# Attention rounds of a fused attention and MoE kernel: the quads' projections one round later, key steps alone in the first two rounds, and unused products behind the routing table

## The chip, the cores and the metric

The kernel runs on one core of a Trainium2 chip. The time is the device time of one execution in microseconds. Three runs of the kernel before took 760.27, 762.58 and 767.11 us; the median is 762.58. A further execution was profiled: it took 762.83 us, and its span from the first to the last instruction is 761.1 us.

## The reference, cut to what matters

Three layers follow each other. The part that the change touches is the first, a linear attention with the feature map exp(p), exp(-p) of a projection p from which its largest magnitude is taken; and, at its end, the start of the second, a mixture of 8 experts with one expert per token.

```python
def phi(x):                                   # x is q or k: 4 batches, 8 heads, 576 tokens, 64
    proj = np.einsum('bhsd,df->bhsf', x, w_phi)                # 64 -> 128 features
    proj = proj - np.max(np.abs(proj), axis=-1, keepdims=True)
    return np.concatenate([np.exp(proj), np.exp(-proj)], axis=-1)
q_p, k_p = phi(q), phi(k)
kv = np.einsum('bhsf,bhsd->bhfd', k_p, v)
z = np.sum(k_p, axis=2)
num = np.einsum('bhsf,bhfd->bhsd', q_p, kv)
den = np.einsum('bhsf,bhf->bhs', q_p, z)[..., None] + 1e-06
x = num / den                                 # 2304 tokens of 512, then:
logits = normalized(x) @ normalized(expert_emb).T / tau       # 8 experts; argmax picks one
...
out[mask] = gate_w[mask, None] * (np.maximum(x[mask] @ w1[e], 0.0) @ w2[e])   # per expert
h = np.maximum(np.maximum(x @ m1, x @ m2), x @ m3); return h @ w_out          # third layer
```

## The kernel before

The attention is written out by hand in program order; every engine runs its instructions in that order, and waits on semaphores. Its loop runs over 18 *rounds* (`for r in range(R1)`, line 488). Two streams run through the rounds:

- **Key steps.** The keys and values are cut into 18 steps (`steps`): for each batch two row blocks (`u`) by two halves of the heads (`hq`), and for each pair of batches one step for the rows that are left. Step n goes through `k_T` (PE transposes, ACT copies to `kT`), `k_proj` (PE products with w_phi into two PSUM banks `pskp`), `k_exp` (DVE takes the largest magnitude `mk` and subtracts it to `pk`; ACT makes two exps, `kp`), `k_pair` (DVE adds the two rows of a pair, `zr`) and `k_acc` (PE sums key-value products `kv` and key sums `z`). In round r, step r is summed, step r+1 projected and step r+2 transposed.
- **Quads of queries.** The queries are cut into 16 quads (4 per batch; two share one load `q`). A quad goes through `q_T` (PE transposes, DVE copies to `qT`), `q_front` (PE products `psqf`, ACT copies them to `pq`, POOL's all-reduce over the partitions gives the maxima `mq`), `q_sub` (DVE subtracts), `q_exp` (ACT, to `ex`) and, once its batch's keys are summed, `q_num` and, every second quad, `q_den`. The dictionary `at` says in which round a quad's `q_num` stands: quads 0 to 7 in rounds 5 to 12, quads 8 on from round 14. `LEAD = 4` puts `q_front` four rounds ahead of it, `q_exp` three, and `q_T` five.

Names of PSUM tiles made by `bank(...)` share five banks in turn (tag `W`), so a PE instruction that writes a bank waits until the reader of the tile five places back is done. `idle(n)` issues n products of zeros into a bank that nobody reads; before the loop 11 of them stand ahead of the first transposes, 8 in round 0. `prep_experts` (the generator `pe`) normalizes the expert embeddings `emb` on DVE ahead of the first key step and transposes them in round 2 (`ps_en`, to `enp`). Loads are issued on SP in program order (`load_u` keys and values, `load_r` the left rows, `load_q`), a few first ones on ACT; w_phi is loaded twice, into both halves of `w2`.

Behind the loop comes the tail: the last quads, then the routing generator `chain` (`Routing.blocks`): PE products `rt_n`, `rt_before`, and 18 products of 18 columns, `rt_tok`, in three groups, each waiting for a table `R` that DVE makes. DVE casts the result to the token list `s2t`, and POOL gathers token rows `xs` by it from DRAM, where the x tiles were stored. The expert layer begins with `fill(12)` twice (line 1035): 24 unused products of 512 columns, then the transposes of the gathered rows (`turn`, line 933).

Of the kernel before, what the change touches and what calls it, by code (L numbers as in the profile page):

```python
# [46 lines left out]
def attention(tc, q, k, v, w_phi, expert_emb, tau, x_d, lraw, ssq, ident, io, kx, ex_, rt, ids):  # L47
# [17 lines left out]
    LEAD = 4  # L65

    with ExitStack() as ctx:
# [12 lines left out]
        def load_u(b, u, parts=(0, 1)):  # L80
            if (b, u) not in kvu:
                pool = wk if (2 * b + u) % 3 == 1 else io
                kvu[b, u] = pool.tile([P, 2, H, 2, D], F32, tag="kv", name=f"kv{b}_{u}", bufs=1 if pool is wk else 2)
            d = kvu[b, u]
            for i in parts:
                src, dst = ((k, kt), (v, vt))[i]
                for h0, h1 in ((0, 4), (4, 8)) if b == u == i == 0 else ((0, 8),):
                    nc.sync.dma_start(
                        out=d[:, i, h0:h1].rearrange("p h r d -> p h (r d)"),
                        in_=src[b, h0:h1, u * 256:(u + 1) * 256, :].rearrange("h (p r) d -> p h (r d)", r=2),  # L90
                    )
                dst[b, u] = d[:, i]
# [44 lines left out]
        nc.scalar.dma_start(out=w2[D:P], in_=w_phi)  # L137
# [8 lines left out]
        load_kv(3)  # L146
        kld = [4]
# [4 lines left out]
        def idle(n):  # L152

            ps = bank("warm")
# [3 lines left out]
        idle(WARM[4])  # L158
# [14 lines left out]
        def prep_experts():  # L173
# [7 lines left out]
            nc.vector.tensor_tensor(ern, ern, esq, op=ALU.mult)  # L181
            nc.vector.tensor_scalar(ern, ern, 1e-6, taub, op0=ALU.add, op1=ALU.mult)
# [130 lines left out]
        def q_T(v):  # L313
            m, g = divmod(v, 2)
            if g == 0 and m + 1 < 2 * B:
                load_q(m + 1)
            qT[v] = wk.tile([P, 4, 2, QR], F32, tag="qT", name=f"qT{v}")
            for rp in range(2):
# [5 lines left out]
                nc.vector.tensor_copy(qT[v][:, :, rp, :], psv)  # L324

# [158 lines left out]
        k_proj(0)  # L484
        for _ in k_exp(0):
            pass
        fin = None
        for r in range(R1):

            if r + LEAD in at:  # L490
                q_front(at[r + LEAD])
            if r + LEAD - 1 in at:
                m, g = divmod(at[r + LEAD - 1], 2)
                for pp in range(2):
                    q_exp(m * NP_ + 2 * g + pp)
            k_proj(r + 1)

            k_T(r + 2)
            ke = k_exp(r + 1)
            next(ke, None)  # L500
            if r and r + LEAD + 1 in at:
                q_T(at[r + LEAD + 1])
# [11 lines left out]
            for _ in pe if r == 2 else ():  # L514
                pass
            if r == 0:
                idle(8)
            if r + LEAD in at:
                q_sub(at[r + LEAD])
# [26 lines left out]
            if r == 0:  # L546
                q_T(at[LEAD + 1])
            k_pair(r + 1)
# [52 lines left out]
        ex_.low(1, 1)  # L601
        for _ in chain:
# [802 lines left out]
```

## Time and profile before

| | |
|---|---|
| median of the runs | 762.58 us (760.27 to 767.11) |
| profiled execution: time, span | 762.83 us, 761.1 us |
| busy: PE, DVE, ACT, POOL | 734.4, 403.4, 353.4, 135.6 us |
| granted TensorE clock, mean of the span | 0.993 |
| DMA, mean over the span | 100 GB/s |
| attention (to the end of rt_tok) | about 206 us |

How to read it: a timeline row names an engine, a source line, the operation and its tiles; a number in brackets is the time that the engine stood idle just before, with what ended it. A row with x32 covers 32 records; a product of fp32 leaves two records. The granted clock is 1.00 at the upper of its two levels and 0.50 at the lower one. An idle time costs something only where the engine is the one that sets the pace, and in this kernel that is mostly PE.

### The profile page before, as it was taken

The numbers are of one execution on the slowest core, as the hardware profiler recorded it, in microseconds if no ns is written. First come the engines' busy times: TensorE is split into PE (matmuls) and PEld (weight loads), VectorE is DVE, ScalarE is ACT, GpSimd is POOL, SyncE is SP. The second block draws the span as 40 slices with busy tenths as digits, with TensorE's granted clock in tenths as the row PEclk, the third lists the DMA queues.
The fourth block names the chain that finished last, engine by engine and source line by source line (L and its number), as shares of the span: only waits on it lengthen the run. The fifth ranks groups of instructions, "written<-read, shape, count | busy, mean of one in ns | idle before, by whom it ended". The sixth has DMA issues, their size and how long they took to land. (4 is left out here: it accounts for less than half of the span.)

```text
span 761.1 us, 13360 instructions
## 1 busy us (share of the span) xinstructions
PE 734.4 (96%) x5492; PEld 605.0 (79%) x5492; DVE 403.4 (53%) x619; ACT 353.4 (46%) x600; POOL 135.6 (18%) x112
## 2 busy tenths in 40 slices
PE   7899999899999999999999999999999999999995
PEld 6566665665599889998899997888888887888884
DVE  7876667677755554665365588667512222222220
ACT  4676757776755545755275565433231131012111
POOL 1654224442052101005500000000020011002002
PEclk9999999999999999999999999999999999999998
DMA  8644533026147642473334514341010000001001
GB/s 191 156 104 99 112 95 86 16 84 222 72 115 281 229 156 80 176 223 112 113 113 146 190 59 164 122 157 57 2 56 28 1 28 31 0 1 57 0 1 55
DMA packets 59741, 75.93 MB, mean 100 GB/s; under 512 B 11632, under 2 KB 41976, under 8 KB 59648
## 3 DMA queue, kind: packets, MB, share of 16 engines
q1 hardware_dynamic: 55712, 64.53, 27.2%
q0 software_dynamic: 3456, 9.46, 3.6%
q8 instruction: 70, 1.15, 0.7%
q10 hardware_dynamic: 480, 0.61, 0.2%
q14 instruction: 23, 0.19, 0.1%
HBM read 65.12 MB, written 9.46 MB: 98 GB/s over the span
## 5 line engine op out<-in xcount | busy, mean ns | idle before, releaser
L1260 DVE TENSOR_TENSOR raw<-raw,b 128x512 f32<-128x512 f32 x36 | 24.8, 688 | 130.4 <-PE b L1252 126.8
L341 POOL PARTITION_ALL_REDUCE mq<-pq x32 | 69.0, 2206 | 97.5 <-ACT pq L339 91.4
L1281 POOL DMA_INDIRECT out_dram<-raw,c2t x18 | 17.8, 989 | 362.5 <-ACT raw L1280 332.5
L1006 PE MATMUL b<-hxH,wL 128*128 128x304 f32 (+2 forms) x256 | 80.3, 313 | 0.0
L1006 PE MATMUL b<-hxH,wH 128*128 128x304 f32 (+2 forms) x256 | 80.2, 313 | 0.0
L1006 PE MATMUL b<-hxL,wH 128*128 128x304 f32 (+2 forms) x256 | 80.0, 313 | 0.0
L995 DVE SCALAR_TENSOR_TENSOR hxL<-b,hxH 128x512 fp32r<-128x512 f32 x64 | 42.3, 686 | 68.0 <-ACT hxH L994 67.6
L994 ACT ACTIVATE hxH<-b 128x512 fp32r<-128x512 f32 x64 | 38.2, 608 | 44.2 <-PE b L987 40.0
L987 PE MATMUL b<-xeH,w1hi 128*128 128x304 f32 (+2 forms) x256 | 57.2, 317 | 0.0
L987 PE MATMUL b<-xeH,w1lo 128*128 128x304 f32 (+2 forms) x256 | 55.7, 313 | 0.0
L1006 PEld LDWEIGHTS b<-hxL,wH 128*128 128x128 f32 x256 | 48.4, 189 | 2.7 <-DVE hxL L995 0.2
L1006 PEld LDWEIGHTS b<-hxH,wH 128*128 128x128 f32 x256 | 48.4, 189 | 2.6 <-issue 0.2
L1006 PEld LDWEIGHTS b<-hxH,wL 128*128 128x128 f32 x256 | 48.5, 189 | 2.5
L987 PEld LDWEIGHTS b<-xeH,w1lo 128*128 128x128 f32 x256 | 42.0, 189 | 2.9 <-ACT xeH L941 0.4
L987 PEld LDWEIGHTS b<-xeH,w1hi 128*128 128x128 f32 x256 | 41.9, 189 | 2.3
L958 DVE TENSOR_TENSOR wL<-raw,wH 128x2048 fp32r<-128x2048 f32 x16 | 36.6, 2289 | 11.4 <-ACT wH L957 11.4
L987 PE MATMUL b<-xeL,w1hi 128*128 128x304 f32 (+2 forms) x128 | 40.1, 313 | 0.0
L987 PE MATMUL b<-xeL,w1lo 128*128 128x304 f32 (+2 forms) x128 | 39.5, 312 | 0.0
L927 POOL DMA_INDIRECT xs<-x_d,s2t x18 | 21.8, 1212 | 98.6 <-PE b L933 67.6
L1264 ACT CAST m2h<-raw 128x512 fp32r<-128x512 f32 x12 | 7.4, 620 | 67.6 <-DVE raw L1260 67.6
L228 DVE TENSOR_REDUCE mk<-pskp 128x4 f32<-128x512 f32 x36 | 24.7, 685 | 24.8 <-PE pskp L217 24.8
L1252 PE MATMUL b<-xeH,wH 128*128 128x512 f32 x96 | 37.3, 389 | 0.0
(254 smaller groups left out, 1765.3 us busy)
## 6 DMA issues: line engine op xcount, KB each, us to landing
raw<-in_moe_w_dram SPq DMA_DIRECT2D x32, 1024.0 KB
raw<-in_moe_w_dram SPq DMA_DIRECT2D x18, 512.0 KB
q<-in_q_dram SPq DMA_DIRECT2D x8, 576.0 KB
kv<-in_v_dram SPq DMA_DIRECT2D x8, 512.0 KB
x_d<-x SPq DMA_DIRECT2D x16, 256.0 KB
kv<-in_k_dram SPq DMA_DIRECT2D x7, 512.0 KB
raw<-in_moe_w_out_dram SPq DMA_DIRECT2D x6, 512.0 KB
kv<-in_k_dram SPq DMA_DIRECT2D x2, 256.0 KB
```

The lines of the kernel that those rows point to most:

```text
L228: nc.vector.tensor_reduce(m, psb[j], axis=AX.X, op=ALU.max, apply_absolute_value=True)
L341: nc.gpsimd.partition_all_reduce(mx.rearrange("p a b -> p (a b)"), d.rearrange("p a b -> p (a b)"), P, ReduceOp.absmax)
L927: self.nc.gpsimd.indirect_dma_start(out=d, out_offset=None, in_=self.x_d, in_offset=bass.IndirectOffsetOnAxis(ap=idx, axis=0))
L958: self.nc.vector.tensor_tensor(L, r, H.bitcast(F32), op=ALU.subtract)
L987: nc.tensor.matmul(ps[:, 0:N], w, x[:, k, 0:N], start=(i == 0), stop=(i == 11))
L994: nc.scalar.activation(hH, ps, AF.Relu)
L995: nc.vector.scalar_tensor_tensor(hL, ps, 0.0, hH.bitcast(F32), op0=ALU.max, op1=ALU.subtract)
L1006: nc.tensor.matmul(ps[:, 0:N], w[i][:, c:c + P], h[f // 4][:, f % 4, 0:N], start=(f == 0 and q == 0), stop=(f == 7 and q == 2))
L1252: nc.tensor.matmul(b, w, y[k], start=(k == 0 and q == 0), stop=(k == 3 and q == 2))
L1260: nc.vector.tensor_tensor(m, m, b, op=ALU.max)
L1264: nc.scalar.copy(hH, m)
L1281: nc.gpsimd.indirect_dma_start(out=self.out, out_offset=bass.IndirectOffsetOnAxis(ap=rt.c2t[:, t:t + 1], axis=0), in_=o, in_offset=None)
```

## The change

1. **Quads one round on.** `LEAD` goes. In round r the quad is `qv = r - 2`: its `q_front` and `q_sub` stand there, the `q_exp` of quad r-3, the `q_T` of quad r-1. For quads 0 to 7 that is a round later than before; quads 8 to 15 keep their rounds, and round 9, which had no projection, now has quad 7's.
2. **The first two rounds.** Key projections 0 and 1 and transposition 2 stand ahead of the loop; round 0 projects step 2 in the middle of `k_exp(1)`, behind the 8 unused products, and transposes step 3 at its end. Round 1 has `k_pair(1)` in the middle of `k_exp(2)`, and quad 0's `q_T` at its end.
3. **Expert embeddings.** `prep_experts` stops ahead of the step that needs tau; the scaling follows in round 1, the transposes in round 2.
4. **Loads.** The second half of w_phi is loaded on SP behind the first half of the first keys, no longer on ACT. Queries 1 are loaded ahead of the loop, queries m+2 behind the last transposition of queries m.
5. **Unused products.** Those ahead of the first transposes and of round 0 write the bank `kv1` and not one of the five; 12 new ones stand behind the third group of `rt_tok`.

```diff
-    LEAD = 4
...
+                    if h1 == 4:
+                        nc.sync.dma_start(out=w2[D:P], in_=w_phi)
...
-        nc.scalar.dma_start(out=w2[D:P], in_=w_phi)
...
+        load_q(1)
...
-        def idle(n):
-            ps = bank("warm")
+        def idle(n, early=False):
+            ps = ps1.tile([P, 512], F32, tag="kv1", name="warm") if early else bank("warm")
...
-        idle(WARM[4])
+        idle(WARM[4], True)
...
             nc.vector.tensor_tensor(ern, ern, esq, op=ALU.mult)
+            yield
             nc.vector.tensor_scalar(ern, ern, 1e-6, taub, op0=ALU.add, op1=ALU.mult)
...
-            if g == 0 and m + 1 < 2 * B:
-                load_q(m + 1)
...
+            if g == 1 and m + 2 < 2 * B:
+                load_q(m + 2)
...
         k_proj(0)
+        k_proj(1)
+        k_T(2)
...
         for r in range(R1):
-            if r + LEAD in at:
-                q_front(at[r + LEAD])
-            if r + LEAD - 1 in at:
-                m, g = divmod(at[r + LEAD - 1], 2)
+            qv = r - 2
+            if 0 <= qv < NV:
+                q_front(qv)
+            if qv > 0:
+                m, g = divmod(qv - 1, 2)
                 for pp in range(2):
                     q_exp(m * NP_ + 2 * g + pp)
-            k_proj(r + 1)
-            k_T(r + 2)
+            if r > 1:
+                k_proj(r + 1)
+                k_T(r + 2)
             ke = k_exp(r + 1)
             next(ke, None)
-            if r and r + LEAD + 1 in at:
-                q_T(at[r + LEAD + 1])
+            if r == 0:
+                idle(8, True)
+                k_proj(2)
+            elif r == 1:
+                k_pair(1)
+            elif qv + 1 < NV:
+                for _ in pe:
+                    pass
+                q_T(qv + 1)
...
-            for _ in pe if r == 2 else ():
-                pass
-            if r == 0:
-                idle(8)
-            if r + LEAD in at:
-                q_sub(at[r + LEAD])
+            if 0 <= qv < NV:
+                q_sub(qv)
...
             if r == 0:
-                q_T(at[LEAD + 1])
-            k_pair(r + 1)
+                k_T(3)
+            else:
+                if r == 1:
+                    q_T(0)
+                    next(pe)
+                k_pair(r + 1)
...
         next(chain)
         ex_.low(1, 1)
+        idle(12)
         for _ in chain:
```

The order of the instructions, in three places. DVE, from the end of `prep_experts` to quad 0's first copy, before (`mk` and `pk` are a key step's maxima and differences, `qT` a quad's transposed queries):

```order
L182 TENSOR_SCALAR ern<-ern,taub 8x1
L183 RECIPROCAL ern<-ern 8x1
L184 TENSOR_SCALAR emb<-emb,ern 8x512
L228 TENSOR_REDUCE mk_0_226<-pskp_0_215 128x4
L230 TENSOR_TENSOR pk_0_228<-pskp_0_215,mk_0_226 128x512
L228 TENSOR_REDUCE mk_1_232<-pskp_1_216 128x4
L230 TENSOR_TENSOR pk_1_234<-pskp_1_216,mk_1_232 128x512
L228 TENSOR_REDUCE mk_0_256<-pskp_0_238 128x4
L230 TENSOR_TENSOR pk_0_258<-pskp_0_238,mk_0_256 128x512
L228 TENSOR_REDUCE mk_1_262<-pskp_1_239 128x4
L230 TENSOR_TENSOR pk_1_264<-pskp_1_239,mk_1_262 128x512
L324 COPY qT_306<-psqT_0_307 128x4x72
```

DVE in the changed kernel, from the third key step to the scaling of emb and the pair sum `zr` of step 2; the two key steps ahead of it follow the normalization directly:

```order
L230 TENSOR_REDUCE mk_0_321<-pskp_0_270 128x4
L232 TENSOR_TENSOR pk_0_323<-pskp_0_270,mk_0_321 128x512
L243 TENSOR_TENSOR zr_327<-kp_254 128x1024
L230 TENSOR_REDUCE mk_1_329<-pskp_1_271 128x4
L232 TENSOR_TENSOR pk_1_331<-pskp_1_271,mk_1_329 128x512
L324 COPY qT_358<-psqT_0_359 128x4x72
L324 COPY qT_358<-psqT_1_365 128x4x72
L184 TENSOR_SCALAR ern<-ern,taub 8x1
L185 RECIPROCAL ern<-ern 8x1
L186 TENSOR_SCALAR emb<-emb,ern 8x512
L243 TENSOR_TENSOR zr_374<-kp_320 128x1024
```

The tau step, the reciprocal and the scaling stood ahead of the first key reduction and now stand behind three key steps; quad 0's copies went from behind step 1 to behind step 2.

PE from the unused products of round 0 to quad 0's projection, before (`kv`, `z` the sums of a key step, `psqT` and `psqf` a quad's transposes and products):

```order
L156 MATMUL warm<-wz 128x256 x8
L269 MATMUL kv_0_277<-kp_225,kv_0_94 32x256 x16
L274 MATMUL z_279<-kp_225,ones 32x256 x8
L322 MATMUL psqT_0_307<-ident,q_100 128x72 x4
L322 MATMUL psqT_1_313<-ident,q_100 128x72 x4
L335 MATMUL psqf_0_322<-qT_306,w_89 128x288
L335 MATMUL psqf_1_323<-qT_306,w_89 128x288
L335 MATMUL psqf_0_331<-qT_306,w_89 128x288
L335 MATMUL psqf_1_332<-qT_306,w_89 128x288
```

PE in the changed kernel, from the products of key step 0 to quad 0's projection:

```order
L271 MATMUL kv_0_286<-kp_241,kv_0_93 32x256 x16
L276 MATMUL z_288<-kp_241,ones 32x256 x8
L208 MATMUL pskT_313<-ident,kv_1_97 128x128 x4
L271 MATMUL kv_1_287<-kp_254,kv_0_93 32x256 x16
L276 MATMUL z_288<-zr_327,ones 32x256 x4
L322 MATMUL psqT_0_359<-ident,q_100 128x72 x4
L322 MATMUL psqT_1_365<-ident,q_100 128x72 x4
L337 MATMUL psqf_0_377<-qT_358,w_89 128x288
L337 MATMUL psqf_1_378<-qT_358,w_89 128x288
L337 MATMUL psqf_0_386<-qT_358,w_89 128x288
L337 MATMUL psqf_1_387<-qT_358,w_89 128x288
L219 MATMUL pskp_0_394<-w_89,kT_318 128x128
```

Between the products of step 0 and quad 0's projection there stood only quad 0's transposes; now step 3's transposes and the products of step 1 stand there too.

PE at the end of the routing table, before:

```order
L725 MATMUL rt_tok<-ohb,R_2804 128x18 x6
L725 MATMUL rt_tok<-ohb,R_2812 128x18 x6
L725 MATMUL rt_tok<-ohb,R_2827 128x18 x6
L1035 MATMUL b_2884<-w1lo_2569 128x512
L1035 MATMUL b_2885<-w1lo_2569 128x512
```

and in the changed kernel:

```order
L738 MATMUL rt_tok<-ohb,R_2804 128x18 x6
L738 MATMUL rt_tok<-ohb,R_2812 128x18 x6
L738 MATMUL rt_tok<-ohb,R_2827 128x18 x6
L157 MATMUL warm<-wz 128x256 x12
L1048 MATMUL b_2897<-w1lo_2569 128x512
L1048 MATMUL b_2898<-w1lo_2569 128x512
```

The twelve new products of 256 columns stand between the last table product and the 24 of 512 columns, and nothing else moved there.

## Rows read from the trace of the kernel before

**Rows 1.** The page, part 1: busy time, share of the span and instructions of each engine.
```profile
PE 734.4 (96%) x5492; PEld 605.0 (79%) x5492; DVE 403.4 (53%) x619; ACT 353.4 (46%) x600; POOL 135.6 (18%) x112
```

**Rows 2.** Stretches (rounds 1 to 4, 9): length; busy PE, PEld, DVE, ACT, POOL; clock; DMA share, GB/s.
```profile
16.23:21.94 5.71, 5.71 (x76) 4.21 (x77) 4.48 (x7) 3.04 (x7) 1.59 (x1) 1.00 0.92 229
21.94:33.45 11.51, 8.20 (x85) 5.16 (x81) 9.89 (x13) 7.63 (x15) 7.74 (x4) 0.85 0.85 188
33.45:39.21 5.76, 5.76 (x81) 4.23 (x77) 4.64 (x8) 4.92 (x11) 4.13 (x2) 1.00 0.01 3
39.21:50.65 11.44, 11.03 (x153) 7.21 (x149) 8.21 (x13) 7.83 (x17) 4.39 (x3) 1.00 0.57 145
...
91.52:101.48 9.96, 8.82 (x118) 5.92 (x116) 9.44 (x23) 5.02 (x10) 0.00 (x0) 1.00 0.40 86
```

**Rows 3.** Timeline of PE, 0 to 60 us: start, duration, what, idle before and its end.
```profile
6.93 2.05 PE L217 MATMUL pskp<-w,kT 64*128 64x128 f32 x30 [0.65 <-DMA w<-in_w_phi_dram]
...
10.57 1.19 PE L156 MATMUL warm<-wz 128*128 128x256 f32 x8 [1.00 <-DVE pk L230]
...
26.16 0.70 PE L322 MATMUL psqT<-ident,q 72*128 72x72 f32 x8 [0.97 <-DMA q<-in_q_dram]
29.15 0.39 PE L188 MATMUL ps_en<-ident,emb 8*128 8x8 f32 x4 [2.29 <-DVE pk L230]
29.46 3.32 PE L269 MATMUL kv<-kp,kv 128*32 128x256 f32 x32
...
34.52 1.38 PE L217 MATMUL pskp<-w,kT 64*128 64x128 f32 x16
...
36.32 0.67 PE L322 MATMUL psqT<-ident,q 72*128 72x72 f32 x8
36.91 1.93 PE L269 MATMUL kv<-kp,kv 128*32 128x256 f32 x32
```

**Rows 4.** Stretches with granted clock (the number behind the engines): rounds 2 to 3, fill.
```profile
29.00:34.00 5.00, 4.85 (x48) 2.62 (x50) 4.08 (x10) 2.31 (x4) 0.68 (x1) 0.66 0.47 99
...
207.00:211.00 4.00, 4.00 (x12) 3.17 (x11) 0.00 (x0) 1.99 (x2) 2.32 (x3) 0.57 0.19 56
```

**Rows 5.** Timeline of DVE, first four rounds.
```profile
8.20 0.20 DVE L182 TENSOR_SCALAR ern<-ern,taub 8x1 f32<-8x1 f32 x1 [1.05 <-DMA taub<-in_moe_tau_dram]
...
9.03 0.67 DVE L228 TENSOR_REDUCE mk<-pskp 128x4 f32<-128x512 f32 x1
...
15.36 0.82 DVE L324 COPY qT<-psqT 128x288 f32<-128x288 f32 x2 [0.82 <-PE psqT L322]
16.09 1.22 DVE L241 TENSOR_TENSOR zr<-kp 128x1024 f32<-128x1024 f32 x1
...
22.54 1.88 DVE L348 TENSOR_TENSOR pq<-pq,mq 128x576 f32<-128x576 f32 x1 [0.61 <-POOL mq L341]
...
26.46 1.21 DVE L241 TENSOR_TENSOR zr<-kp 128x1024 f32<-128x1024 f32 x1
...
39.11 1.42 DVE L348 TENSOR_TENSOR pq<-pq,mq 128x576 f32<-128x576 f32 x2
```

**Rows 6.** Timeline of POOL, first four rounds.
```profile
20.35 9.32 POOL L341 PARTITION_ALL_REDUCE mq<-pq  x4 [6.06 <-ACT kT L208]
35.08 4.26 POOL L341 PARTITION_ALL_REDUCE mq<-pq  x2 [5.40 <-ACT pq L339]
```

**Rows 7.** Timeline of ACT, rounds 3 and 4.
```profile
34.29 1.31 ACT L339 COPY pq<-psqf 128x288 f32<-128x288 f32 x4 [2.04 <-PE psqf L335]
...
40.31 1.32 ACT L339 COPY pq<-psqf 128x288 f32<-128x288 f32 x4
```

**Rows 8.** Timeline of PE, unused products of round 4, and behind rt_tok.
```profile
45.69 1.21 PE L156 MATMUL warm<-wz 128*128 128x256 f32 x8
...
206.16 7.32 PE L1035 MATMUL b<-w1lo 128*128 128x512 f32 x24 [0.42 <-DVE ne L732]
213.32 0.60 PE L933 MATMUL b<-ident,xs 128*128 128x128 f32 x4
```

## The prediction

> **What bounds the kernel now.** The page's first part comes first: TensorE is busy 96% of the span [rows 1]. A change gains only where PE stands idle, works at the half clock, or does work that can go. Next come the stretches by round [rows 2]. A round is counted from one quad's projection to the next, or in round 9, which has none, from the key projection. Rounds 1 and 3 are full of PE work and take 5.71 and 5.76 us. Round 2 holds the same kinds of work plus four tiny transposes and takes 11.51 us, of which PE is busy 8.20.
>
> Then PE's timeline says what ended each idle time [rows 3]: 0.65 us for the second half of w_phi, 1.00 in front of the unused products of round 0 (for a bank that DVE reads), 0.97 for queries 1, and 2.29 before the emb transposes, again a bank that DVE still reads. After that wait the clock falls: from 29 to 34 us the granted share is 0.66 [rows 4], the lower of the two levels (1.2 GHz of 2.4) for the middle of it, and a key step's 32 records of key-value products take 3.32 us that take 1.93 in round 3 [rows 3]. So 5 x 0.34 = 1.7 us of round 2 is the clock.
>
> Why DVE is late stands in its own timeline [rows 5]. In round 0 it waits 1.05 us for tau and scales emb before its first key reduction starts at 9.03. In round 1 it waits for POOL's maxima, and its subtraction then takes 1.88 us; two of them take 1.42 together in round 4. POOL's first four all-reduces run without pause from 20.35 to 29.67, four microseconds behind the projection that feeds them [rows 2, 6].
>
> **The sum, by rounds.** I compare the instant at which quad 0's projection starts in the changed kernel with the start of round 2 before: by then both have done key steps 0 and 1 and projected keys 0 to 2, and the change has one quad projection and one query transposition less behind it.
>
> *Start to round 2.* w_phi's second half now follows the first half of the keys on SP, so the 0.65 us should go; the second half of the keys gets behind it and may take some tenths back. Key projection 0 has 14 of its 16 records left at 6.93; I let it end at 7.3 instead of about 7.9. The tau wait and the scaling of emb move behind round 1, so DVE starts at 7.3, not 9.03. From there DVE is the path: the reductions and subtractions of three key steps, 12 at 0.67 us = 8.0; one pair sum, 1.22; the two copies of qT, 0.82 [rows 5]. That is 17.4 at the earliest. ACT's exps must free buffers twice and PE's transposes must come in front of the copies, so I take 18.5; the lower end is 17.4, the upper end 20.1 (one idle of 1.00 and one of 0.65, the size of those that go, come back on top of 18.5). Against 21.94: **3.4 us gained**, between 1.8 and 4.5.
>
> *Round 2.* PE's work there is a quad projection 1.07 (33.45 to 34.52), key projection and transposes 1.80 (34.52 to 36.32), query transposes 0.59 (36.32 to 36.91), the emb transposes 0.39, and the step's products 2.3 (36.91 to the next round at 39.21) [rows 2, 3]: 6.1 us. DVE's is four reductions and subtractions 2.7, qT 0.82, the pair sum 1.22, two subtractions of maxima 1.42 [rows 5]: 6.2. I take 6.3, a little above both. Below it stands round 3's 5.76; above it 8.7, if both subtractions cost 1.88 as at 22.54. Queries 1 are first needed a round later; their load stands at the same place of SP's queue as before, so "moved up" itself gives nothing, and the 0.97 goes because the reader is later. With no idle of 2.29 I expect no fall of the clock here. Against 11.51: **5.2 us gained**, between 2.8 and 5.7.
>
> *Rounds 3 and 4.* Same work as before. But ACT needs 6.02 us from one quad's copies to the next, with hardly a pause, more than PE's 5.76. Before, it entered round 3 having waited 2.04 us [rows 7]; now the rounds ahead are shorter and it enters without that lead, so the banks of the quad projections come free late and the key projection behind them waits. **1.0 us lost**, between 0 and 2.0 (the lead of 2.04 gone altogether).
>
> *Round 9.* The projections of quads 0 to 7 stand a round later, so round 9 gets a quad projection (1.07) and rounds 8 and 9 together one more query transposition (0.59): 1.66 us of PE, of which little is covered, since round 9 had only 1.1 us idle in 9.96 [rows 2]. **1.3 us lost**, between 0.8 (most of that idle covers it) and 1.66. Rounds 5 to 8 and 10 to 17 keep their work and their place; nothing.
>
> *Behind rt_tok.* Twelve unused products at 0.15 (1.21 for 8) are 1.8 us at the full clock, in place of an idle of 0.42 [rows 8]: the 24 products behind them start 1.4 later. They took 7.16 us (206.16 to 213.32) [rows 8], and from 207 to 211 the clock was granted 0.57 [rows 4], so 4 x 0.43 = 1.7 of it is the half clock. If the new products keep the clock up, the end is 0.3 earlier; if it falls all the same, 1.4 later. In the trace it fell although 1.2 us of dense products stood ahead of the fall, and the sparse stretch before (the 18-column products of rt_tok) is unchanged. I take **0.4 lost**, between 0.3 gained and 1.4 lost. The gathered rows cannot bring more: PE turns them without idle at 213.32, and the trace shows no more than that they had landed.
>
> Other moves: one DMA issue less on ACT is covered by PE, for which ACT's first copy waits. The load of queries m+2 stands behind a transposition it must wait for anyway; behind it on SP stand key loads and x stores of the same round, which are due later. Nothing for both.
>
> Sum: 3.4 + 5.2 - 1.0 - 1.3 - 0.4 = 5.9 us, against the profiled execution's 762.83: 756.9. The median of the runs is 0.25 below that execution, so I give **756.7**. All terms at their best give 4.5 + 5.7 - 0 - 0.8 + 0.3 = 9.7, at their worst 1.8 + 2.8 - 2.0 - 1.66 - 1.4 = -0.5.
>
> **A row and a rule.** Subtracting the maxima costs 1.88 us where an all-reduce runs beside it from the start [rows 5, 6]; the one at 39.11 overlaps the last 0.2 us of an all-reduce (35.08 + 4.26) and costs no more than the usual half of 1.42. By the trace such a meeting costs 1.1 us. The Trainium skill, "SBUF — State Buffer", section on who interferes with whom, says that a DVE instruction with two SBUF inputs and a GpSimd instruction that reads SBUF exclude each other, and that the second to start blocks fully. By that rule a meeting would cost up to the rest of an all-reduce, some 2.1 us by its row (4.26 for two), and the pair sum would be open to it too; the trace has a pair sum of ordinary length (the one at 26.46, inside POOL's 9.32 us) that speaks against the whole of it. It gives rival 2.
>
> **Rivals.**
> 1. *The waits move instead of going* (18%). ACT and DVE, not PE, end every early round: round 2 lasts 8.7, quad 0's projection starts at 20.1. Gain 1.8 + 2.8 - 1.0 - 1.3 - 0.4 = 1.9, so 760.7. For it: DVE's 6.2 and ACT's 6.02 both exceed PE's 5.76. Against: in rounds 3 and 4, with the same load, PE hardly waits [rows 2].
> 2. *Slower* (6%). DVE, no longer held up by other work, reaches the subtraction while POOL still reduces that quad, in rounds 2, 3 and 4 alike; the first all-reduce cannot start much before 20.35 if the 6.06 us idle in front of it are POOL's own. Two subtractions a round that are each held up by the length of an all-reduce, 9.32 / 4 = 2.3 us [rows 6], are 4.6 us on DVE; less the 1.1 us that it stands idle in a round such as 3 (4.64 busy of 5.76) [rows 2], 3.5 us a round and 10.5 in three: 756.7 + 10.5 = 767.2. It decides when the second all-reduce of a quad ends more than a few tenths behind DVE's arrival. In the trace quad 0's subtraction met one, the one in round 4 all but missed it [rows 5]. Later rounds have the slack to hide it.
> 3. *Nothing comes back* (16%). ACT keeps up in rounds 3 and 4, the start goes as DVE's sum says, the clock holds behind rt_tok: 4.5 + 5.2 - 0 - 1.3 + 0.3 = 8.7 us gained, 753.9. For it: PE's waits in rounds 3 and 4 are small now. Against: the lead of 2.04 us that ACT had there [rows 7].
>
> **Chances.** Forecast 60% with its own range 754.5 to 759.5; rivals 18, 6 and 16%. One per cent, about what a measurement of this kernel can tell from no change, is 7.6 us, so faster by over 1% means under 754.95: three quarters of rival 3 and a tenth of the forecast, 18%, and a little for causes I do not see: 0.20. Slower by over 1%, over 770.2, needs rival 2 with every term at its worst: 0.03. Within: 0.77. The range goes past rival 3 below and just past rival 1 above: 753.5 to 761.2, which leaves out rival 2 and the ends of the others.
>
> **What would show it.** Right: quad 0's projection between 17.4 and 20 us; granted clock 1.00 through the first 60 us; no PE idle over 1 us from 6 us to round 4 except in front of quad 0's projection; round 2 near 6.3; round 9 about a microsecond longer; round 4 a little longer than 11.44, with PE's waits ended by ACT's pq. Wrong: subtractions of maxima at 1.9 us in rounds 3 and 4 (rival 2), round 2 over 8 us (rival 1), or a fall of the clock in the first two rounds, where the work is now key steps with transposes and little else. Behind rt_tok, the clock of the 24 products decides the last term.

## The result, and the profile after

| | before | after |
|---|---|---|
| median of 8 runs | 762.67 us (760.27 to 767.11) | 756.60 us (754.79 to 757.94) |
| profiled execution: time, span | 762.83, 761.1 us | 756.55, 754.8 us |

The ratio is 0.9913, with a 95% interval of 0.9887 to 0.9939: 6.1 us less, within 1% of before. The forecast was 756.7.

The page's first part answers to [rows 1]: TensorE (PE) does 2.0 us less of busy time, in a span that is 6.3 us shorter. The rest, 4.3 us, was waiting.

```profile
PE 732.4 (97%) x5504; PEld 605.9 (80%) x5504; DVE 401.1 (53%) x619; ACT 352.5 (47%) x600; POOL 135.7 (18%) x112
```

The stretches of rounds 2, 3, 4 and 9 (length; busy time of PE, PEld, DVE, ACT, POOL; granted clock; DMA) answer to [rows 2].

```profile
18.67:25.02 6.35, 6.35 (x80) 4.59 (x80) 5.83 (x13) 3.24 (x8) 4.43 (x2) 1.00 1.02 226
25.02:31.04 6.02, 5.95 (x80) 4.22 (x77) 5.91 (x10) 6.02 (x14) 4.39 (x2) 1.00 0.97 203
31.04:42.22 11.18, 10.89 (x152) 7.21 (x148) 8.02 (x13) 7.57 (x16) 4.61 (x3) 1.00 0.83 177
83.10:94.00 10.90, 9.88 (x126) 6.99 (x124) 10.02 (x25) 7.25 (x16) 4.26 (x2) 1.00 0.19 55
```

Round 2 took 11.51 us with PE idle for 3.31 of them and a clock of 0.85; now PE is busy for all of its 6.35 and the clock is 1.00. Round 9 has the projection that it lacked and is 0.94 longer. Rounds 3 and 4 together take 17.20 us in both.

PE's timeline, first rounds, answers to [rows 3]. Behind the unused products at its start, only two idle times of over half a microsecond are left in the first 34 us: 1.25 us for the second half of the first keys, and 0.66 in front of quad 0's projection.

```profile
5.95 0.66 PE L208 MATMUL pskT<-ident,kv 128*128 128x128 f32 x4 [1.25 <-DMA kv<-in_k_dram]
6.54 2.06 PE L219 MATMUL pskp<-w,kT 64*128 64x128 f32 x32
...
18.67 1.24 PE L337 MATMUL psqf<-qT,w 64*128 64x288 f32 x8 [0.66 <-DVE qT L324]
...
21.58 0.41 PE L190 MATMUL ps_en<-ident,emb 8*128 8x8 f32 x4
...
22.73 1.93 PE L271 MATMUL kv<-kp,kv 128*32 128x256 f32 x32
```

DVE's and POOL's timelines answer to [rows 5, 6]. Here is the change at its core: POOL's all-reduces come in pairs with a pause of 1.93 us between the pairs, and DVE's two subtractions of quad 0, 1.42 us together, fall into the pause. Quad 1's two start 0.7 us before POOL is done with it (26.65 + 4.73 = 31.38), and take 1.49.

```profile
7.73 0.69 DVE L230 TENSOR_REDUCE mk<-pskp 128x4 f32<-128x512 f32 x1 [0.58 <-PE pskp L219]
...
24.70 1.42 DVE L350 TENSOR_TENSOR pq<-pq,mq 128x576 f32<-128x576 f32 x2
...
30.68 1.49 DVE L350 TENSOR_TENSOR pq<-pq,mq 128x576 f32<-128x576 f32 x2
```

```profile
20.29 4.43 POOL L343 PARTITION_ALL_REDUCE mq<-pq  x2 [7.52 <-ACT pq L341]
26.65 4.73 POOL L343 PARTITION_ALL_REDUCE mq<-pq  x2 [1.93 <-ACT pq L341]
```

Behind rt_tok [rows 4, 8], PE's timeline and then the stretches with the clock (the number behind the engines) show that the twelve new products did not keep the clock up in this execution.

```profile
197.56 0.84 PE L738 MATMUL rt_tok<-ohb,R 128*128 128x18 f32 x6 [0.62 <-DVE R L694]
198.25 2.44 PE L157 MATMUL warm<-wz 128*128 128x256 f32 x12
200.80 6.42 PE L1048 MATMUL b<-w1lo 128*128 128x512 f32 x24
207.06 0.60 PE L946 MATMUL b<-ident,xs 128*128 128x128 f32 x4
```

```profile
199.00:201.00 2.00, 1.90 (x9) 1.63 (x9) 0.50 (x5) 0.44 (x3) 0.00 (x0) 0.50 0.01 1
201.00:203.00 2.00, 2.00 (x7) 1.58 (x8) 0.00 (x0) 1.84 (x2) 1.30 (x1) 0.69 0.00 0
```

### The profile page after: what moved, and what is told of

Its sections match the earlier page's. It is cut to its first block, busy times and chain, and to the rows that moved or that the text cites. A ratio compares the mean times of both kernels' runs of the same rounds, so it can differ in the third digit from the quotient of the medians.

```text
span 754.8 us, 13386 instructions
## 1 busy us (share of the span) xinstructions
PE 732.4 (97%) x5504; PEld 605.9 (80%) x5504; DVE 401.1 (53%) x619; ACT 352.5 (47%) x600; POOL 135.7 (18%) x112
## 5 line engine op out<-in xcount | busy, mean ns | idle before, releaser
L1265 PE MATMUL b<-xeH,wL 128*128 128x512 f32 x96 | 37.3, 389 | 0.0
```

The costliest lines, as they stand in the source:

```text
L1265: nc.tensor.matmul(b, w, y[k], start=(k == 0 and q == 0), stop=(k == 3 and q == 2))
```

## The experiments

The runs came in three groups, each with its own runs of before. A difference below is taken against the before of the same group, or between kernels of one group where it says so.

| kernel | median us | before in its group | ratio, 95% interval |
|---|---|---|---|
| without the twelve products | 755.76 | 762.99 | 0.9914 (0.9900 to 0.9928) |
| quads early again | 764.46 | 762.99 | 1.0014 (0.9996 to 1.0033) |
| before, quads late only | 759.62 | 762.99 | 0.9956 (0.9940 to 0.9972) |
| before, an all-reduce ahead | 765.85 | 762.99 | 1.0049 (1.0032 to 1.0065) |
| quads early, no maxima of quad 0 | 761.08 | 763.69 | 0.9966 (0.9948 to 0.9984) |
| before, quads late, q loads up | 757.37 | 763.69 | 0.9923 (0.9900 to 0.9946) |
| without products, emb back | 755.85 | 763.69 | 0.9901 (0.9880 to 0.9923) |
| without products, w_phi back | 756.14 | 763.69 | 0.9917 (0.9891 to 0.9943) |
| the changed kernel again | 757.59 | 763.55 | 0.9908 (0.9878 to 0.9939) |
| products in the gaps | 755.21 | 763.55 | 0.9884 (0.9856 to 0.9913) |
| without products, 16 for 24 | 755.60 | 763.55 | 0.9889 (0.9859 to 0.9918) |
| the same, w_phi behind the keys | 755.12 | 763.55 | 0.9885 (0.9857 to 0.9914) |

### What made round 2 long

**Quads early again.** The changed kernel with `q_front`, `q_exp`, `q_sub` and `q_T` of quads 0 to 7 a round earlier.

```diff
-            qv = r - 2
-            if 0 <= qv < NV:
-                q_front(qv)
...
+            if r + 4 in at:
+                q_front(at[r + 4])
...
                 k_T(3)
+                q_T(0)
```

> The changed kernel with quads 0 to 7 (projections, maxima, transpositions) a round earlier again, as before the change; key projections a step ahead, the late scaling of emb, w_phi on SP and the twelve products stay. Theory: the quad in round 1 is what made round 2 long, since the POOL maxima of quad 0 cannot begin before about 20.3 us and DVE stands behind them; the long round 2 comes back (8 to 11 us for 6.35), round 9 gets its 0.94 back: 759 to 761 against 756.6. Rival: key projections a step ahead are what brought the gain; then only round 9 changes and it is 755.7.

The time is 764.46 us, even above the 759 to 761 that the theory gave; the rival's 755.7 is out. Of this kernel the timelines of POOL, DVE and PE:

```profile
19.40 9.37 POOL L343 PARTITION_ALL_REDUCE mq<-pq  x4 [6.82 <-ACT pq L341]
```

```profile
22.26 1.85 DVE L350 TENSOR_TENSOR pq<-pq,mq 128x576 f32<-128x576 f32 x1
24.38 1.86 DVE L350 TENSOR_TENSOR pq<-pq,mq 128x576 f32<-128x576 f32 x1 [0.27 <-POOL mq L343]
...
26.57 1.45 DVE L186 TENSOR_SCALAR emb<-emb,ern 8x512 f32<-8x512 f32 x1
27.95 1.21 DVE L243 TENSOR_TENSOR zr<-kp 128x1024 f32<-128x1024 f32 x1
```

```profile
17.81 1.96 PE L337 MATMUL psqf<-qT,w 64*128 64x288 f32 x8 [0.75 <-DVE qT L324]
...
22.64 1.24 PE L337 MATMUL psqf<-qT,w 64*128 64x288 f32 x8
...
28.17 0.38 PE L190 MATMUL ps_en<-ident,emb 8*128 8x8 f32 x4 [2.54 <-DVE emb L186]
30.63 0.72 PE L322 MATMUL psqT<-ident,q 72*128 72x72 f32 x4 [1.68 <-DVE pk L232]
31.27 3.64 PE L271 MATMUL kv<-kp,kv 128*32 128x256 f32 x32
```

The two projections stand 4.83 us apart, and a quad needs 4.4 us of POOL and then 1.4 of DVE. So POOL goes from one quad into the next without pause, and both subtractions start 0.13 or 0.14 us behind the start of an all-reduce (at 22.12 the second of quad 0, at 24.25 the first of quad 1) and take 1.85 us each, not 0.71. DVE then scales emb late, PE waits 2.54 and 1.68 us, the clock falls, and 32 products take 3.64 us that take 1.93 at the upper level. Round 2 is 13.06 us long (22.64 to 35.70). Note that POOL was in time here: its first all-reduce began at 19.40, right behind the first copies (by ACT's timeline three of them ran from 18.56 to 19.56).

**An all-reduce ahead of POOL's iotas**, in the kernel before.

```diff
+        dm = cp.tile([P, 8], F32, tag="dm", name="dm")
+        nc.vector.memset(dm, 0.0)
+        nc.gpsimd.partition_all_reduce(dm, dm, P, ReduceOp.absmax)
         rt.prep(QR)
```

> The kernel before with one added instruction: an all-reduce of 128x8 zeros on POOL ahead of its iotas, whose result nothing reads. Theory: the first all-reduce of a program is late for a reason of POOL's own (it began at 20.35, some 2.7 us behind the copy that feeds it, while in the changed kernel it began 0.2 us behind its copy); paid early, quad 0's maxima begin near 17.8 us, DVE's wait and PE's idle of 2.29 go with the half clock, and the time is 758 to 760 against 762.7. Rival A: the lateness stays (the iotas behind it make POOL start anew); 762.7 or slower. Rival B: the maxima come early but the subtractions are slow all the same (1.88 us), and only 1 us is gained.

Rival A held, and the time rose by 0.5%. The first all-reduce of a quad came 6.84 us behind the last iota (6.06 in [rows 6]) and 3.2 us behind the copies it reads, though another had run already. Rows of ACT and of POOL:

```profile
19.06 1.31 ACT L342 COPY pq<-psqf 128x288 f32<-128x288 f32 x4 [1.30 <-PE psqf L338]
```

```profile
22.92 9.32 POOL L344 PARTITION_ALL_REDUCE mq<-pq  x4 [6.84 <-ACT kT L211]
```

What the delay comes from stays open; the order iota, then all-reduce, shows it in both kernels, and that the gap stays with the iotas ahead speaks for a change of POOL's work, not for a first use. It did not test what it was made for, since it did not bring the maxima forward. In the experiment before they were in time, and the round was long all the same; but there the quads also followed each other more closely than in the kernel before. Whether maxima in time would have been enough in the kernel before, no run shows.

**Quads early, without the maxima of quad 0.** Its subtractions take zeros, so that this quad's features are computed without their maxima.

```diff
...
+                if v == 0:
+                    pq[u], mq[u] = d, mz.unsqueeze(2).to_broadcast([P, 2, SH])
+                    continue
                 mx = wk.tile([P, 2, SH], F32, tag="mq", name=f"mq{u}", bufs=3)
```

> The kernel of the previous experiment with quads 0 to 7 a round early (764.5), with one thing left out: quad 0's two all-reduces on POOL; its subtractions take zeros instead, so that the scaling of the first eighth of the queries isn't computed as it should be. Theory: what makes the early quad costly is that DVE reaches quad 0's subtraction while POOL still reduces (POOL runs 19.40 to 28.77 without pause there, two subtractions of 1.85 each, PE 2.54 and 1.68 idle, then the half clock). Without POOL in quad 0 the subtractions take 1.42 together, round 2 is about 6.3, the clock holds and the time is 756 to 757.5. Rival: DVE and ACT have too much to do in rounds 1 and 2 with the quad there, whoever they wait for; then round 2 stays over 9 us and the time over 760.

Round 2 shrank as the theory said, from 13.06 to 6.45 us, with no wait on PE. But the time is 761.08, scattered from 757.85 to 763.31, not 756 to 757.5. In the profiled execution the clock fell a round earlier: of PE's rows, the 32 products of round 1 took 3.44.

```profile
20.07 3.44 PE L271 MATMUL kv<-kp,kv 128*32 128x256 f32 x32
...
23.88 1.24 PE L337 MATMUL psqf<-qT,w 64*128 64x288 f32 x8
...
30.33 1.24 PE L337 MATMUL psqf<-qT,w 64*128 64x288 f32 x8
```

So what POOL does for quad 0 is shown to make round 2 long in the kernel with quads early. But the early quad has a further cost of some 4 us, of which the fall in round 1 is a part. That the short products there, with a pause of 0.76 us in front, bring the fall, and that falls make the scatter of the runs, is argued, not shown: in the kernel that has the maxima too, the same products stood behind a pause of 0.75 us, and the 32 behind them took 1.93.

### Which parts of the change brought the time

**Quads late, nothing else**, and **quads late with the loads of queries moved up**, both on the kernel before. The second diff comes on top of the first.

```diff
-            if r + LEAD in at:
-                q_front(at[r + LEAD])
...
+            qv = r - 2
+            if 0 <= qv < NV:
+                q_front(qv)
...
-            if r == 0:
-                q_T(at[LEAD + 1])
+            if r == 1:
+                q_T(0)
```

> The kernel before with one part of the change alone: quads 0 to 7 a round later. Key projections not ahead, emb scaled ahead of the first reduction, w_phi on ACT's queue, no products behind rt_tok. Theory: this part carries most of the gain: round 2 about 6.3 to 7 us for 11.51, round 9 a microsecond longer, the start some 1 to 2 us shorter since a quad's projection and transposition have left it; 757.5 to 759 against 762.7. Rival: without the projections a step ahead DVE waits for each key projection in rounds 0 to 2 and the start is as long as before; 760 to 761.

```diff
+        load_q(1)
         kld = [4]
...
-            if g == 0 and m + 1 < 2 * B:
-                load_q(m + 1)
...
+            if g == 1 and m + 2 < 2 * B:
+                load_q(m + 2)
```

> The kernel with quads 0 to 7 a round late and nothing else (759.6), and beside it the loads of queries moved up as in the change. In the other the second load of queries was issued a round later with its transposition, and round 3 waited 1.22 us for it (7.12 us long for 6.02). Theory: the wait goes and with it 1.1 us: 758.5. Rival, my prediction's reading that moving the loads up gives nothing: 759.6.

Late alone gives 3.4 us; late with the loads up 6.3. The first, 759.62, lies between what its theory and its rival gave; the second, 757.37, is a microsecond under its theory. In the first, a row of PE in round 3 shows why:

```profile
31.83 0.69 PE L322 MATMUL psqT<-ident,q 72*128 72x72 f32 x8 [1.22 <-DMA q<-in_q_dram]
```

The load of queries 1 was issued together with quad 0's transposition. A round later it was a round late (issued from 21.09 us on, not at 17.79). Moved up, round 3 is 5.71 us long for 7.12. That is 1.4 of the 2.5 us by which the ratios differ; the rest the profiles don't separate. These two moves alone give as much as the whole change, which also bears the cost of the products behind rt_tok.

**Emb scaled first again**, and **w_phi's second half on ACT again**, both without the twelve products.

```diff
             nc.vector.tensor_tensor(ern, ern, esq, op=ALU.mult)
-            yield
             nc.vector.tensor_scalar(ern, ern, 1e-6, taub, op0=ALU.add, op1=ALU.mult)
...
                     q_T(0)
-                    next(pe)
```

> The changed kernel without the twelve products (755.8), with the scaling of emb put back ahead of DVE's first key reduction. Theory: DVE is the path of the first 18 us; it waits for tau (which landed between 8.2 and 10.2 us in the runs so far) and scales for 0.8 us, so that its first reduction starts at 9.0 or later for 7.5, and all behind it moves by 1.3 to 2 us: 757.1 to 757.8. Rival: ACT's exponentials and PE have as much to do, and DVE's start is hidden; under 0.5 us lost.

```diff
-                    if h1 == 4:
-                        nc.sync.dma_start(out=w2[D:P], in_=w_phi)
...
         nc.scalar.dma_start(out=w2[0:D], in_=w_phi)
+        nc.scalar.dma_start(out=w2[D:P], in_=w_phi)
```

> The changed kernel without the twelve products (755.8), with the second half of w_phi back on ACT's queue. Theory: the move took away a wait of 0.65 us at the first key projection and delayed the second half of the keys by 1.3 us (5.95 for 4.63); the first reduction came at 7.5 to 7.7 after, and would at 8.0 to 8.3 with the half back, since the projection of the first keys needs all of w_phi: 756.1 to 756.4. Rival: the second keys come sooner and the projection of them, which is what DVE needs next, makes up for it: 755.5 to 755.8.

In the first the rival's number holds, but not its reason. Tau was there by 7.33 us (ACT issued its load at 2.07 us, at 2.71 in the kernel before), so the first reduction came at 8.15, only some 0.4 to 0.7 us behind that of the kernels without this edit (7.73, 7.47); quad 0's projection came as much later, 19.07 for 18.67 and 18.40, so nothing hid it, and the median shows nothing. The second is undecided: PE waited 1.34 us for w_phi, and the second keys came without a wait; the median, 756.14, lies in the theory's range, but only 0.3 above the other of the same group, within the scatter. A row of DVE of the first, a row of PE of the second:

```profile
8.15 0.67 DVE L229 TENSOR_REDUCE mk<-pskp 128x4 f32<-128x512 f32 x1
```

```profile
7.05 3.38 PE L218 MATMUL pskp<-w,kT 64*128 64x128 f32 x30 [1.34 <-DMA w<-in_w_phi_dram]
```

What key projections a step ahead bring is seen on DVE. From its first reduction to quad 0's projection it takes 10.91 to 10.94 us in seven executions that have them and no fall of the clock in between (7.73 to 18.67 in the changed kernel), and 11.47 with quads late alone, which has them not: half a microsecond. The other kernel without them, with the loads up, took 12.49, but in that execution the lower clock lasted into this stretch, as a row of PE shows that takes 0.66 at the upper level:

```profile
12.11 1.11 PE L207 MATMUL pskT<-ident,kv 128*128 128x128 f32 x4
```

In one group of runs, the rest of the change (with emb back and without the products) is 1.5 us under the two moves alone, 755.85 for 757.37; the intervals of the ratios overlap.

### Behind rt_tok

**Without the twelve products**, and **the changed kernel again**.

```diff
         ex_.low(1, 1)
-        idle(12)
         for _ in chain:
```

> The changed kernel without the twelve unused products behind rt_tok, nothing else. Theory: they only displace. The clock fell behind rt_tok with them as without them, and they put the first transposition of gathered rows 1.1 us later after rt_tok's end (8.92 against 7.84). Without them the transposition starts about 1.1 us earlier and the time is 755.5 against 756.6. Rival A: without them the half clock lasts longer by what they would have cost; no change, 756.6. Rival B: the gathered rows, which had landed 1.7 us ahead of the transposition, now come last; then less than 1.1 comes back. A gain over 2 us would say that the products had themselves caused the fall.

> The changed kernel itself, once more, beside the three that follow. 755.5 to 757.5 (medians of before have moved by 1 us from one group of runs to the next). Behind rt_tok the first transposition of gathered rows stood 8.0 to 8.4 us behind the start of rt_tok's last group where the clock held, and 9.4 where it fell, with the twelve products; 7.1 and 8.4 without. Which of the two this execution shows is open: of three profiled executions with them the clock fell in one, of seven without in six.

The first is 7.2 us under its before, the changed kernel 6.1 and, again, 6.0; the intervals of the ratios overlap, and the profiles below tell more.

**Six products in the idle times**, and **16 for 24 of the products behind**.

```diff
+        idle(4)
         next(chain)
         ex_.low(1, 1)
-        idle(12)
+        idle(2)
```

```diff
         ex_.low(1, 1)
-        idle(12)
...
         fill(12)
         nxt, idx0 = regs(0), index(0, ET.PE, ET.Activation, ET.DVE)
-        fill(12)
+        fill(4)
```

> The changed kernel with its twelve unused products behind rt_tok replaced by four in the idle of 0.62 us ahead of rt_tok's last group and two in the idle of 0.42 behind it. Theory: what the twelve cost is that they stand in front of 24 products that do the same for the clock; in the gaps they cost nothing: 1 us under the changed kernel in the same group of runs, whether or not the clock falls. Rival: dense products all through the stretch keep the clock, which the twelve behind it could not; then 1.3 us more comes back, 2.3 under it, and the profile shows no half clock from 195 to 205.

> The changed kernel without the twelve products, and with 16 for 24 of the unused products behind them. Theory: the gathered rows have landed 3.6 us behind the issue of their gather, at about 204.1 with the issue at 200.5, while PE turned them at 205.7; the 24 products are now the longer path where the clock falls, and hardly where it holds (206.21 there, behind a landing near 205.9). 8 products less give 1.2 to 1.7 us in the first case and 0.3 in the second: 1.5 to 2.5 under the changed kernel in the same runs. Rival: the first of the products that follow wait for the weights or for rows behind the first two; then nothing comes on top of the 1 us for the twelve.

One table holds them all: the time from the start of rt_tok's last group to the first transposition of gathered rows, in the profiled executions. (One is left out: with the loads of queries up, the clock fell for longer and it took 9.77.)

| | clock fell | clock held |
|---|---|---|
| no products, 24 behind | 8.42 (before), 8.43, 8.45, 8.39, 8.39 | 7.11 |
| twelve products, 24 behind | 9.50 (after), 9.51 | 8.03, 8.04 |
| six in the gaps, 24 behind | | 7.11 |
| no products, 16 behind | 7.10, 7.13 | |

The twelve cost 1.07 us where the clock falls and 0.93 where it holds. The fall itself costs 1.3 to 1.5. And 8 products less give back as much as a clock that holds. The last row and the second cell of the first end at the same 7.1 us, so something else bounds there: the gathered rows. PE's rows of the kernel with 16, with its idle of 0.37 in front of the transposition:

```profile
198.90 0.84 PE L737 MATMUL rt_tok<-ohb,R 128*128 128x18 f32 x6 [0.63 <-DVE R L693]
200.16 5.47 PE L1047 MATMUL b<-w1lo 128*128 128x512 f32 x16 [0.42 <-DVE ne L744]
206.00 0.63 PE L945 MATMUL b<-ident,xs 128*128 128x128 f32 x4 [0.37 <-issue]
```

The gather was issued at 202.1. By an estimate from the median of such gathers in the kernel with w_phi back, 3.6 us from issue to landing, the rows were there at 205.7. In the kernel with 16 products and w_phi behind the keys (below), PE's second transposition waits for a gather by name:

```profile
206.88 0.66 PE L945 MATMUL b<-ident,xs 128*128 128x128 f32 x4 [0.21 <-DMA xs<-x_d,s2t]
```

Against the changed kernel in the same group the medians are 2.0 us lower (16 products) and 2.4 (products in the gaps). The latter's profiled execution kept the clock through the stretch:

```profile
197.89 0.71 PE L157 MATMUL warm<-wz 128*128 128x256 f32 x4
198.66 0.84 PE L739 MATMUL rt_tok<-ohb,R 128*128 128x18 f32 x6
199.35 0.48 PE L157 MATMUL warm<-wz 128*128 128x256 f32 x2
199.93 5.73 PE L1049 MATMUL b<-w1lo 128*128 128x512 f32 x24
205.77 0.63 PE L947 MATMUL b<-ident,xs 128*128 128x128 f32 x4
```

The rival's signs are there, but one execution does not show that the gaps keep it. Of its six runs three, the profiled one among them, have a mean granted clock of 0.998, and three 0.994 or 0.995; the changed kernel has 0.998 in three of 14. The mean is a weak sign, since it is over the whole span and so holds other falls too: in the profiled execution it is 0.54 from 750 us on, where PE is done. Whether filled gaps make a fall rarer stays open.

**w_phi behind both halves of the first keys**, with 16 products.

> The kernel of the previous run (16 unused products behind rt_tok) with the second half of w_phi behind both halves of the first keys on SP, not between them. Theory: the second keys then land at 4.6 again, as before the change, and w_phi before PE needs it: the first DVE reduction comes 0.3 to 0.6 us earlier and the time is that much lower. Rival: w_phi now lands as late as the second keys did, PE waits as long, one instruction later; no difference within 0.2 us.

```diff
-                    if h1 == 4:
+                    if b == u == i == 0 and h1 == 8:
                         nc.sync.dma_start(out=w2[D:P], in_=w_phi)
```

PE transposes both halves without a wait and then waits 0.23 us, for ACT, not for w_phi:

```profile
4.08 1.50 PE L208 MATMUL pskT<-ident,kv 128*128 128x128 f32 x8
5.81 2.06 PE L219 MATMUL pskp<-w,kT 64*128 64x128 f32 x32 [0.23 <-ACT kT L210]
```

The first reduction starts at 7.31, against 7.47 and 7.73 in the two executions above that project the first keys at the upper clock and scale emb late (the kernel without products and the changed kernel): 0.16 and 0.42 us, for the theory's 0.3 to 0.6. The median is 0.5 us lower than the run beside it, which the intervals don't separate. At 755.12 this is the lowest median of the versions, 2.5 us under the changed kernel in the same group (755.10 to 758.17 there, 754.59 to 755.50 here).

## Why the prediction was right, point by point

| step | forecast us | measured us |
|---|---|---|
| start to round 2 | 3.4 gained (1.8 to 4.5) | 3.27 gained (21.94 to 18.67) |
| round 2 | 5.2 gained (2.8 to 5.7) | 5.16 gained (11.51 to 6.35) |
| rounds 3 and 4 | 1.0 lost (0 to 2.0) | 0 (17.20, 17.20) |
| round 9 | 1.3 lost (0.8 to 1.66) | 0.94 lost |
| behind rt_tok | 0.4 lost (0.3 gained to 1.4 lost) | 1.08 lost (8.42 to 9.50 from the start of rt_tok's last group) |

The sum was 5.9, and it is 6.3 by the spans; the rest of the program moved by less than 0.3 us in all. That the median fell within 0.1 us of the forecast is partly luck: rounds 3, 4 and 9 came out 1.4 us better than their terms and the stretch behind rt_tok 0.7 worse, and the same kernel's second median is 757.59.

*Start to round 2.* DVE was the path as forecast. The 18.5 were made of a first reduction at 7.3 and 10.1 us of DVE's work, with about a microsecond on top; it was 7.73 and 10.94. The step that failed in it is w_phi: its 0.65 us went, but the second half of the keys lost 1.25, not "some tenths" (0.71 to 1.25 in the profiled executions with w_phi between the halves), and putting w_phi back changed nothing in the median that the scatter lets one see. Part of the term is the execution's own: in the repeat of the changed kernel quad 0's projection came at 19.88, since the first key projection took 3.38 us there and not 2.06.

*Round 2.* The length was right, and so were the signs (no long idle, no slow subtraction, no fall of the clock). Its reason was right only in part. The prediction put weight on POOL's lateness of four microseconds; with POOL in time, but projections only 4.83 us apart, the round was 13.06 us. What counts is where in POOL's work on a quad DVE's subtractions fall, and two things move that. One is POOL's start: in the kernel before, where the projections stood 5.71 us apart, it was late, and in round 3 there, with projections 5.76 apart and POOL in time, the subtractions at 39.11 were not held up. The other is the distance of the projections, which no term of the prediction asked for. That POOL's lateness alone made round 2 long in the kernel before stays argued. The 0.97 us for queries 1 went as told: SP issued their load at 17.77 (17.79 before), and its reader on PE came at 28.12, not at 26.16 after its wait. But a later reader alone would not have done it: with the load tied to it, as before, it waited 1.22. The load had to be taken off that reader to stay where it was. The sentence that moving the loads up "itself gives nothing" holds against before, and misled: by the two kernels above, a change without it would have been some 2.5 us slower.

*Rival 2* had the right price and the wrong place. A meeting costs 1.85 - 0.71 = 1.1 us, twice per quad, and it struck where quads stood early, not in rounds 2 to 4 of the changed kernel; in all of that kernel only the last quad's first subtraction, at 171.31, takes 1.85. What neither the rival nor "A row and a rule" asked is which of the two starts first, and by how much. All the slow ones start 0.12 to 0.14 us into an all-reduce. In round 3 of the changed kernel one starts 1.52 us into an all-reduce and takes its ordinary 0.75, and the pair sum at 27.95 in the kernel with quads early starts 1.57 us into one (26.38) and takes its ordinary 1.21. Rows of DVE and POOL in the changed kernel:

```profile
30.68 0.75 DVE L350 TENSOR_TENSOR pq<-pq,mq 128x576 f32<-128x576 f32 x1
```

```profile
26.65 2.61 POOL L343 PARTITION_ALL_REDUCE mq<-pq  x1 [1.93 <-ACT pq L341]
29.16 2.22 POOL L343 PARTITION_ALL_REDUCE mq<-pq  x1
```

Where DVE starts first, POOL pays. The pair sum at 26.46 before, which the prediction read as a sign against the rule, started 0.22 us ahead of POOL's fourth all-reduce, and that one took 3.00 us, not 2.22; the first row of POOL above, 2.61, began 0.61 us behind the start of the pair sum at 26.04.

```profile
26.68 3.00 POOL L341 PARTITION_ALL_REDUCE mq<-pq  x1
```

By the Trainium skill, "SBUF — State Buffer", section "Who interferes with whom", issue order decides which of the two is blocked, and the trace agrees. It does not agree with a block to the end of the all-reduce, the price that the prediction drew from the rule: a subtraction that starts at 0.13 and takes 1.85 for 0.75 was held up to some 1.2 us behind the start of an all-reduce of 2.2, by an estimate from these rows.

*Rounds 3 and 4.* The mechanism came as told: ACT was busy for all of round 3's 6.02 us, and the round was 0.26 longer than before. The size was wrong: round 4 gave it back (11.18 for 11.44), since with 7.57 us of work in it ACT has slack there. The lead of 2.04 us was not needed, and the sign named for round 4, a little longer than 11.44, did not come.

*Round 9.* Nearer to the lower end: PE's idle there stayed near 1 us (1.02 for 1.14), so that the projection's 1.07 came on top almost whole, but the query transposition that round 8 got cost nothing there (11.14 us before, 11.15 after).

*Behind rt_tok.* Both branches were sized well: with a fall 1.07 measured for 1.4, and with the clock held 0.39 earlier than before (8.03 for 8.42) for 0.3. The profiled execution took the first. The sentence that the gathered rows "cannot bring more" passed over what was to be had there: by the estimate of 3.6 us they had landed some 1.6 us before PE turned them, in the kernel before (issue at 208.08) and without the products (200.5), and 8 products less brought 1.3 us in the profiled executions.

## What to carry to other kernels

Where two engines handle an item one after the other and disturb each other, count both on one line. Here a quad takes some 4.4 us on POOL and then 1.4 on DVE: with projections 4.83 us apart both subtractions were slowed and everything queued behind them waited; in rounds 2 to 4 of the changed kernel, with POOL in time and projections at least 6.02 apart, none was. When a consumer is moved later, look whether its load is issued with it; a load tied to its reader moves along and the wait comes back. Filler that waits for a transfer should be no longer than the transfer needs, by the landing and not by the idle time that the filler hides.

## What the runs showed of the hardware that was not expected

- Whether the clock falls behind rt_tok differs between executions in which the instructions of this stretch are the same: without the products 8.4 us with a fall in five kernels, 7.1 without in one; with them 9.5 with a fall in two executions, 8.0 without in two.
- Scaling emb, 8 partitions by 512 elements, took 1.45 us where it started 0.2 us into an all-reduce and 0.47 alone, more than the pair sum of 128 by 1024, which started 1.57 us into the same one and took its usual 1.21.
- An all-reduce behind iotas began no sooner than 6.06 and 6.84 us after them in two kernels, also when another all-reduce had run ahead of the iotas.
- The program's start varies too. In the repeat of the changed kernel two of PE's first rows, below, take 1.11 and 3.38 us that take 0.66 and 2.06 in the execution shown first, while the row of the granted clock says 1.00 from 5 to 10 us in both. There the durations, and not that row, tell the level, and 1.3 us of a single execution's time hang on it.

```profile
5.79 1.11 PE L208 MATMUL pskT<-ident,kv 128*128 128x128 f32 x4 [0.85 <-DMA kv<-in_k_dram]
6.83 3.38 PE L219 MATMUL pskp<-w,kT 64*128 64x128 f32 x32
```
